# Attention and MLP block on one core: a written-out order of all work, w1 scaled in place, and k's subtractions on GpSimd

## The chip, the cores and the metric

One core of one Trainium2 chip runs the whole kernel. The metric is device microseconds from launch to end. The engines are PE (TensorE, matmuls and transposes), DVE (VectorE), ACT (ScalarE), POOL (GpSimd) and SP (SyncE, which here only issues DMAs).

## The reference

```python
# q, k, v: [8 batches, 8 heads, 576 rows, 64], float32
q_s = softmax(q, over the 64 columns)
k_s = softmax(k, over the 576 rows)
kv  = einsum('bhsd,bhse->bhde', k_s, v)
x   = einsum('bhsd,bhde->bhse', q_s, kv)      # rearranged to [8, 576, 512]
xn  = (x - mean(x)) / sqrt(var(x) + 1e-6) * g # over the 512 columns
out = x + relu(xn @ w_ch1) @ w_ch2            # w_ch1 [512, 2048], w_ch2 [2048, 512]
```

## The kernel before, in words

**Tiles.** Each batch has 576 rows: four tiles of 128 (J = 4) and 64 rows left over. The left-over rows of two batches share one tile, tile number 4, which is treated with the odd batch. The MLP runs in nine chunks of 512 rows: chunk 0 to 7 for the four full tiles of each batch, chunk 8 for the left-over tiles of all eight.

**One batch (`Side`).** `load_k`, `load_v`, `load_q` and the left-over loads bring 1 MB each, plus 128 KB for left-over rows. For k: `kmax` and `kmaxl` take the maximum over rows within a partition (DVE), `kar` reduces it over partitions (POOL, L182), `ksub` subtracts it in place (two large instructions of 128x1024 and a small one of 64x512, DVE, L200), `kexp` takes the exponential (ACT, L213). `vcast` brings v to bf16 (L100). `pkv` multiplies them (PE, L316) and `kvb` divides by the column sums, which come from a column of ones in v (DVE, L325 and L328). For q: `qmax`, `qsub` (DVE, L262, L267), `qexp` (ACT, L272), a transpose, by PE (`qT`, `qTe`) for batches 0 and 1 and by a DMA transpose (`qTd`, L306) later, and the row sums (`zq`, or `zpe` and `zrec` on PE and DVE for batches 0 and 1). `po` multiplies q by kv (PE, L340), `x` scales by the row sums (DVE, L363), `xn` subtracts the mean, `sq` sums squares (ACT, L394), and `xT` with `xTe`, or the DMA transpose `xTd` (L419), gives x transposed.

**g.** In batches 0 and 1 `xTe` multiplies by g when it leaves PSUM (L413). From batch 2 on `xn` is two DVE instructions: L375 scales the sum to a mean, L376 subtracts it and multiplies by g, which `g_bc` holds on all partitions.

**One chunk.** `l1` is 64 matmuls into 16 blocks (`ph`, L449, and `l1_part`, L463, in smaller pieces for chunks 0 and 1), `relu` moves each block to `hT` (ACT, L455, L470), `l2` adds 64 matmuls into four results (`pc`, L505), `put` scales by the row's 1/std and adds x (DVE, L515), `store` writes it out. Four PSUM tiles serve `mm_ps` (ph, pc), four serve `sm_ps` (everything of the batches).

**Order.** All work is a list of tasks with needs. A planner in the kernel file (`dues`, `forward`) gives each task a due time from set costs and a table of shifts, and writes them in a fixed order per engine. All loads and stores but the last store go through SP's queue, in order; weights go through POOL's queue (`load_w1` L428, `load_w2` L432), each of four parts of w1 and w2 being one DMA. Two gates hold SP's queue: `gate` is a tiny DMA that reads w1's second part, so batch 1's loads stand behind its landing; the second reads w2's last part, and loads of later batches stand behind it. `hold` on POOL waits for batch 1's v before w2 is asked for. Batch 0 takes q in two halves (`HALVED`).

Of the kernel before, what the change touches and what calls it, by code (L numbers as in the profile page):

```python
# [13 lines left out]
FP32 = mybir.dt.float32  # L14
# [7 lines left out]
def kernel(  # L22
# [24 lines left out]
    HALVED = (0,)  # L47
    FIRST_DMA = 2
    ZPE = 2
    EARLY_KL = (("kll", 0), ("kl", 0, 1))  # L50
    WARM = 30
    G0 = 1
# [18 lines left out]
    g_bc = const.tile([P, DM], FP32)  # L71
    gate_sb = const.tile([1, 16], BF16)
    hold_sb = const.tile([1, 16], FP32)
# [19 lines left out]
    xm_ab = const.tile([P, B, J + 1], FP32)  # L93
# [12 lines left out]
    def by_dma(m, j):  # L106
        return m >= FIRST_DMA or j == J

    lefts = {}

    def left_over(ring, tag, src, m):

        if (tag, m // 2) not in lefts:
            lefts[tag, m // 2] = ring.tile([P, H, D], FP32, tag=tag, name=tag)
        nc.sync.dma_start(
            lefts[tag, m // 2][rows(m)], src[m, :, SM:, :].transpose([1, 0, 2])
        )

    class Side:
# [6 lines left out]
        def load_kl(self):  # L126
            left_over(kin, "kl", k, self.m)

        def load_k(self, part, parts):
            if part == 0:  # L130
                self.kt = kin.tile([P, H, J * D], FP32, tag="kt")
            hn = H // parts
            hs = slice(hn * part, hn * part + hn)
            src = k[self.m, :, :SM, :].rearrange("h (p j) d -> p h (j d)", j=J)
            nc.sync.dma_start(self.kt[:, hs], src[:, hs])

        def load_v(self):
            src = v[self.m, :, :SM, :].rearrange("h (p j) d -> p h (j d)", j=J)
            self.vt = vin.tile([P, H, J * D], FP32, tag="vt")
            nc.sync.dma_start(self.vt, src)  # L140

        def load_vl(self):
            left_over(vin, "vl", v, self.m)

        def load_q(self, part):
            if part == 0:
                self.qt = qin.tile([P, H * J * D], FP32, tag="qt")
            if self.halved:
                n = H * 2 * D
                src = q[self.m, :, part * 2 * P:(part + 1) * 2 * P, :]  # L150
                nc.sync.dma_start(
# [3 lines left out]
            else:  # L155
                src = q[self.m, :, :SM, :].rearrange("h (p j) d -> p h (j d)", j=J)
                nc.sync.dma_start(self.qt.rearrange("p (h e) -> p h e", h=H), src)

        def load_ql(self, b):
            left_over(qin, "ql", q, b)  # L160

        def kmax(self, hs):
# [4 lines left out]
            nc.vector.tensor_tensor(  # L167
                kmx[:, hs], kt[:, hs, :2 * D], kt[:, hs, 2 * D:], op=ALU.max
            )
            nc.vector.tensor_tensor(  # L170
# [3 lines left out]
        def kmaxl(self, hs):  # L174
            m = self.m
            kmx, r = self.kmx, rows(m)
            nc.vector.tensor_tensor(  # L177
# [192 lines left out]
        def xn(self, eng, j):  # L370

            xt, xs = self.xs[j]
            if by_dma(self.m, j):
                xm = xm_ab[:, self.m, j:j + 1]
                nc.vector.tensor_scalar_mul(xm, in0=xs, scalar1=INV)  # L375
                nc.vector.scalar_tensor_tensor(  # L376
                    xn_ab[:, j], in0=xt, scalar=xm, in1=g_bc,
                    op0=ALU.subtract, op1=ALU.mult,
                )
            elif eng is nc.scalar:  # L380
# [17 lines left out]
        def xT(self, j):  # L398
            pxt = self.pxt[j] = sm_ps.tile([P, KO1, P], BF16, tag="sm", name="pxt")
            for c in range(KO1):  # L400
                nc.tensor.transpose(
                    pxt[:, c, :], xn_ab[:, j, c * P:(c + 1) * P], ident
                )

        def _xnT(self, j):
            m = self.m
            return (
                xnT_ab[:, self.sl, :, j * P:(j + 1) * P] if j < J
                else xnTl[:, :, (m // 2) * P:(m // 2 + 1) * P]
            )  # L410

        def xTe(self, eng, j):
            eng.tensor_tensor(  # L413
                self._xnT(j), self.pxt[j], g_sb[:, :, None].to_broadcast([P, KO1, P]),
                op=ALU.mult,
            )
# [12 lines left out]

    def load_w2(g4):  # L430
        s = slice(4 * g4, 4 * g4 + 4)
        nc.gpsimd.dma_start(w2_sb[:, s], w2_src[:, s, :])  # L432

    def gate(what, c):

        src = w1_sb[:1, 0, c * DM:c * DM + 16] if what == "w1" else w2_sb[:1, 4 * c, :16]
        nc.sync.dma_start(gate_sb, src)

    def hold():

        nc.gpsimd.tensor_copy(hold_sb, side[1].vt[:1, 0, :16])
# [78 lines left out]
    def store(ci, ti):  # L520
        if ci in HALVED:
            dst = out[ci, (ti // 2) * 2 * P:(ti // 2 + 1) * 2 * P, :]
            nc.sync.dma_start(dst.rearrange("(p j) c -> p j c", j=2)[:, ti % 2, :], ots[ti])
        elif ci < B:
            dst = out[ci, :SM, :].rearrange("(p j) c -> p j c", j=J)
            nc.sync.dma_start(dst[:, ti, :], ots[ti])
        else:
            for b in (2 * ti, 2 * ti + 1):
                nc.sync.dma_start(out[b, SM:, :], ots[ti][rows(b)])
# [4 lines left out]


    PE, DV, AC, PO, SP = "pe", "dve", "act", "pool", "sp"
    ENG = {PE: nc.tensor, DV: nc.vector, AC: nc.scalar, PO: nc.gpsimd, SP: nc.sync}
    RING = {"mm": 4, "sm": 4, "ot": 4}
    LATE = {PE: 0.25, DV: 0.12, AC: 0.12, PO: 0.12, SP: 0.1}
    START = {SP: 1.0, AC: 1.0, PO: 4.0}  # L540
    COLD = 25.0
    HOLD = 3.0
    EARLY = 14
    FIRST, SECOND, PERIOD = 20.0, 52.0, 29.7
    TT, CAST, KAR = 1, 2, 3
    SHIFT = {
        ("qmax", 0, 2): 1.8, ("qsub", 0, 2): 10.5, ("relu", 0, 1, 3): 20.8,
        ("relu", 0, 3, 2): 9.2, ("x", 0, 3): -9.0, ("zq", 0, 1): 20.5, ("kexp", 1, 0): 12.9,
        ("ksub", 1, 0): 10.4, ("ksub", 1, 1): 16.3, ("po", 1, 1): -3.4, ("po", 1, 3): -2.8,
        ("put", 1, 0): 40.7, ("put", 1, 1): 41.6, ("put", 1, 3): 9.5, ("qll", 1, 1): -80.7,  # L550
        ("qmax", 1, 2): 22.9, ("relu", 1, 4, 2): 10.2, ("relu", 1, 5, 0): 9.4,
        ("relu", 1, 5, 2): 120.4, ("relu", 1, 6, 0): 51.3, ("relu", 1, 6, 2): 9.8,
        ("relu", 1, 7, 2): 19.9, ("x", 1, 4): -154.5, ("xT", 1, 1): -16.6, ("xn", 1, 2): 26.9,
        ("zq", 1, 4): 115.1, ("kl", 2, 0): -39.6, ("qexp", 2, 2): -6.4, ("qmax", 2, 2): 13.8,
        ("qsub", 2, 0): -2.4, ("qsub", 2, 2): -26.6, ("relu", 2, 1): 61.2, ("relu", 2, 12): 117.0,
        ("relu", 2, 7): 30.4, ("store", 2, 1): 31.4, ("store", 2, 2): 38.1, ("vl", 2): -23.4,
        ("x", 2, 3): 22.2, ("zq", 2, 0): -13.4, ("kexp", 3, 0): -21.5, ("kl", 3, 0): -30.4,
        ("kmaxl", 3, 0): 6.4, ("ksub", 3, 2): -23.6, ("kvb", 3): -29.9, ("qll", 3, 0): -169.6,
        ("qmax", 3, 2): 59.3, ("relu", 3, 10): 81.4, ("relu", 3, 7): 19.6, ("relu", 3, 8): 124.9,
        ("vl", 3): -7.0, ("zq", 3, 0): 58.2, ("kexp", 4, 0): -17.7, ("kl", 4, 0): 42.8,  # L560
        ("kmax", 4, 0): 75.7, ("ksub", 4, 2): -8.6, ("ql", 4, 0): -52.7, ("qsub", 4, 0): 66.6,
        ("vl", 4): 60.6, ("vll", 4): -50.7, ("kmax", 5, 0): -41.7, ("kmaxl", 5, 0): -34.8,
        ("ksub", 5, 1): -45.8, ("ql", 5, 0): 45.7, ("vl", 5): 44.4, ("kl", 6, 0): 4.8,
    }
    tasks = []

    class Task:
        def __init__(self, due, fn, args, eng, need, after, takes, frees, mlp, move, grain, port):
            self.due, self.fn, self.args, self.eng = due, fn, args, eng
            self.need, self.after, self.takes, self.frees = need, after, takes, frees  # L570
            self.mlp, self.move, self.grain, self.port = mlp, move, grain, port
            self.users = []
            self.n = len(tasks)

    def task(
        fn, args, eng, *need, after=None, takes=None, frees=None, mlp=False, move=None, due=None,
        grain=1.0, port=0,
    ):
        flat = []
        for x in need:  # L580
            flat.extend(x if isinstance(x, (list, tuple)) else [x])
        need = [x for x in flat if x]
        after = [x for x in (after if isinstance(after, list) else [after]) if x]
        t = Task(due, fn, args, eng, need, after, takes, frees, mlp, move, grain, port)
        tasks.append(t)
        return t

    def long(t, e, at):
        w = t.eng[e]
        return 2 * w if e == PE and at < COLD else w  # L590

    def lag(t):

        return (1.9 if t.move else 0.12 if t.on == PE else 0.05)

    class Wire:

        def __init__(self):
            self.now, self.rings = 0.0, {e: [] for e in ENG}

        def run(self, until, rings):
            now = self.now
            while now < until:
                heads = [r for r in rings.values() if r]
                if not heads:
                    return
                now = max(now, min(r[0][2] for r in heads))
                if now >= until:
                    return
                going = [r for r in heads if r[0][2] <= now + 1e-9]  # L610
                whole = sum(r[0][0].grain for r in going)
                dt = min(r[0][1] * whole / r[0][0].grain for r in going)
                for r in heads:
                    if r[0][2] > now + 1e-9:
                        dt = min(dt, r[0][2] - now)
                dt = min(dt, until - now)
                now += dt
                for r in going:
# [548 lines left out]
```

## Time and profile before

| what | value |
|---|---|
| time, median of 3 runs | 308.18 us (307.34 to 309.3) |
| profiled execution, time | 308.83 us |
| profiled execution, span | 307.0 us |
| PE, DVE, ACT, POOL busy | 284.8, 210.2, 161.0, 42.2 us |
| mean granted PE clock | 0.972 |
| DMA moved | 49.90 MB, mean 163 GB/s |

Times inside the profile count from the start of the span. A wait is put down to the work that released the waiting instruction. Where a line of the profile ends in a bracket, it gives idle time before the instruction and its releaser. A suffix "q" (SPq, POOLq) is an engine's queue issuing a DMA.

### The profile page before, as it was taken

The page shows a single profiled execution, that of the slowest core. Times are in us where ns is not written, and L with a number is a line of the kernel's source. Part 1 is how long each engine was busy: PE and PEld are TensorE (multiplying, and loading weights), DVE is VectorE, ACT ScalarE, POOL GpSimd, SP SyncE. Part 2 cuts the span into 40 slices and gives each one's busy share as a digit, 9 for nine tenths or more (in the row PEclk, how much of TensorE's full clock was granted, in tenths as well). Part 3 has the DMA queues.
Part 4 walks back from the last instruction along what each step waited for, and adds up shares of the span by engine and source line. Part 5 has one row for each costly group of instructions (what it writes and reads, how often), then busy time and mean ns, then how long its engine had stood idle before and what let it go on. Part 6 is the DMA issues. An engine that isn't in the chain of part 4 may idle for free.

```text
span 307.0 us, 5187 instructions
## 1 busy us (share of the span) xinstructions
PE 284.8 (93%) x2002; PEld 153.9 (50%) x2030; DVE 210.2 (68%) x347; ACT 161.0 (52%) x288; POOL 42.2 (14%) x46
## 2 busy tenths in 40 slices
PE   6659959999989998999999999999999999999995
PEld 2239955568544444445444545444544444444444
DVE  5893898789888896998889889988984500020012
ACT  1444746459543974286837763777477136106500
POOL 2600150023113000233016100060000000000000
PEclk9956998999999999999999999999999999999999
DMA  6999998999999995599398369945142310010023
GB/s 207 251 184 260 259 182 134 296 275 323 188 240 169 283 213 126 143 270 339 93 275 202 68 160 222 287 55 137 70 87 51 105 69 0 34 70 34 0 65 74
DMA packets 79545, 49.90 MB, mean 163 GB/s; under 512 B 44960, under 2 KB 74912, under 8 KB 79520
## 3 DMA queue, kind: packets, MB, share of 16 engines
q1 hardware_dynamic: 75136, 45.24, 62.1%
q0 software_dynamic: 4224, 4.19, 8.7%
q8 instruction: 16, 0.26, 0.4%
q10 hardware_dynamic: 160, 0.13, 0.2%
q14 instruction: 9, 0.07, 0.1%
HBM read 36.96 MB, written 9.44 MB: 151 GB/s over the span
## 4 chain that ended last, share of the span: by engine, by line
PE 76%; DMA 13%; DVE 3%; ACT 2%; issue 1%; SPq 1%; POOL 1%; ACTq 0%
PE pc L505 36%; PE ph L449 31%; DMA vt<-in_v_dram 4%; PE ph L463 3%; DMA qT_sb<-eq_sb 3%; DMA w_sb<-in_moe_w_ch_dram 3%; DMA kt<-in_k_dram 2%; PE pot L340 2%; DVE v_ab L100 2%; PE pk L316 1%; PE pc L481 1%; ACT ek_ab L213 1%; DMA xnT_ab<-xn_ab 1%; ACT hT L455 1%; POOL km L182 1%
## 5 line engine op out<-in xcount | busy, mean ns | idle before, releaser
L505 PE MATMUL pc<-w_sb,hT 128*128 128x512 bf16 x543 | 124.6, 381 | 1.3 <-issue 0.7
L455 ACT ACTIVATE hT<-ph 128x512 bf16<-128x512 f32 x112 | 66.0, 597 | 58.5 <-PE ph L449 58.1
L449 PE MATMUL ph<-xnT_ab,w_sb 128*128 128x512 bf16 x375 | 84.6, 379 | 0.8 <-DMA xnT_ab<-xn_ab 0.3
L505 PEld LDWEIGHTS <-hT 128*128 128x128 bf16 x560 | 53.8, 98 | 61.7 <-issue 1.4
L449 PEld LDWEIGHTS <-w_sb 128*128 128x128 bf16 x448 | 43.4, 98 | 51.9 <-issue 0.8
L515 DVE SCALAR_TENSOR_TENSOR ot<-pc,rstd,x_ab 128x512 f32<-128x512 f32 x32 | 23.9, 750 | 39.5 <-PE pc L505 37.6
L463 PE MATMUL ph<-xnT_ab,w_sb 128*128 128x128 bf16 (+1 forms) x384 | 31.4, 246 | 1.0 <-DVE xnT_ab L413 1.0
L394 ACT ACTIVATE xsq<-x_ab,xs_ab 128x512 bf16<-128x512 bf16 x32 | 23.0, 718 | 14.8 <-DVE x_ab L363 13.8
L463 PEld LDWEIGHTS <-w_sb 128*128 128x128 bf16 x384 | 29.0, 103 | 2.8 <-issue 0.9
L272 ACT ACTIVATE eq_sb<-qt 128x1024 bf16<-128x1024 f32 (+1 forms) x17 | 17.1, 1005 | 20.3 <-DVE qt L267 18.0
L363 DVE SCALAR_TENSOR_TENSOR x_ab<-pot,rq 128x512 bf16<-128x512 f32 x32 | 21.0, 686 | 7.3 <-PE pot L340 6.9
L100 POOL CAST v_ab<-vt 128x1024 bf16<-128x1024 f32 x12 | 13.1, 1123 | 87.7 <-DMA vt<-in_v_dram 87.7
L470 ACT ACTIVATE hT<-ph 128x512 bf16<-128x512 f32 x32 | 18.3, 593 | 9.1 <-PE ph L463 8.8
L182 POOL PARTITION_ALL_REDUCE km<-kmx x9 | 17.0, 1886 | 36.2 <-DVE kmx L177 34.1
L267 DVE TENSOR_TENSOR qt<-qt,qm 128x1024 f32<-128x1024 f32 (+1 forms) x17 | 20.4, 1208 | 0.3
L262 DVE TENSOR_REDUCE qm<-qt 128x16 f32<-128x1024 f32 (+1 forms) x17 | 19.2, 1146 | 0.6 <-DMA qt<-in_q_dram 0.5
L376 DVE SCALAR_TENSOR_TENSOR xn_ab<-x_ab,xm_ab,g_bc 128x512 bf16<-128x512 bf16 x24 | 18.0, 752 | 0.8
L515 DVE SCALAR_TENSOR_TENSOR ot<-pc,rstd,xl 128x512 f32<-128x512 f32 x3 | 2.3, 750 | 21.9 <-PE pc L505 21.9
L200 DVE TENSOR_TENSOR kt<-kt,km 128x1024 f32<-128x1024 f32 x14 | 17.0, 1237 | 0.1
L213 ACT ACTIVATE ek_ab<-kt 128x1024 bf16<-128x1024 f32 x14 | 14.5, 1052 | 1.6 <-DVE kt L200 1.5
L277 DVE TENSOR_REDUCE sumq<-eq_sb 128x16 f32<-128x1024 bf16 x12 | 14.5, 1204 | 0.1
L449 PE MATMUL ph<-xnTl,w_sb 128*128 128x512 bf16 x62 | 13.9, 379 | 0.1
(73 smaller groups left out, 199.3 us busy)
## 6 DMA issues: line engine op xcount, KB each, us to landing
vt<-in_v_dram SPq DMA_DIRECT2D x8, 1024.0 KB, 9.4
out_dram<-ot SPq DMA_DIRECT2D x32, 256.0 KB, 2.9
kt<-in_k_dram SPq DMA_DIRECT2D x7, 1024.0 KB, 8.1
qt<-in_q_dram SPq DMA_DIRECT2D x7, 1024.0 KB, 8.9
w_sb<-in_moe_w_ch_dram POOLq DMA_DIRECT2D x8, 512.0 KB, 10.0
kt<-in_k_dram SPq DMA_DIRECT2D x2, 512.0 KB, 5.4
kl<-in_k_dram SPq DMA_DIRECT2D x8, 128.0 KB, 6.9
vl<-in_v_dram SPq DMA_DIRECT2D x8, 128.0 KB, 6.6
```

The lines of the kernel that those rows point to most:

```text
L100: eng.copy(dst, src) if eng is nc.scalar else eng.tensor_copy(dst, src)
L182: nc.gpsimd.partition_all_reduce(self.km[:, hs], self.kmx[:, hs, :D], P, bass_isa.ReduceOp.max)
L262: nc.vector.tensor_reduce(t, self._q(a, n), axis=AX.X, op=ALU.max)
L267: eng.tensor_tensor(x, x, t[:, :, :, None].to_broadcast([P, n, H, D]), op=ALU.subtract)
L363: nc.vector.scalar_tensor_tensor(xt.rearrange("p (h d) -> p h d", h=H), in0=self.pot[j], scalar=-1.0, in1=rq[:, :, None].to_broadcast([P, ...
L394: nc.scalar.activation(xsq, xt, AF.Square, bias=xs, scale=-float(DM), accum_out=s)
L449: nc.tensor.matmul(ph, w1_sb[:, ko, m * P:(m + 1) * P], src[:, ko, :], start=(ko == 0), stop=(ko == KO1 - 1),)
L455: nc.scalar.activation(hT[:, m, :], phs[m], AF.Relu)
L463: nc.tensor.matmul(ph[:, i], w1_sb[:, ko, m * P:(m + 1) * P], xnT_ab[:, ci % 2, ko, t * P:(t + n) * P], start=(ko == 0), stop=(ko == KO1 - 1),
L470: nc.scalar.activation(hT[:, c * (4 // n):(c + 1) * (4 // n), t * P:(t + n) * P], phs[c, t], AF.Relu)
L505: nc.tensor.matmul(pcs[ti], hT[:, ko, ti * P:(ti + 1) * P], w2_sb[:, ko, :], start=(ko == 0), stop=(ko == KO2 - 1),)
L515: nc.vector.scalar_tensor_tensor(ots[ti], in0=pcs[ti], scalar=rstd[:, ci, ti:ti + 1], in1=xt, op0=ALU.mult, op1=ALU.subtract,)
```

## The change

The planner, its costs and its shifts go. The order is a written-out list, `PROGRAM`, of task names with the engine where there is a choice; `write_all` follows it word for word. Both gates, `hold`, `g_bc` and the two halves of batch 0's q go. ACT may issue loads and stores too. In chunk 0 g is applied as before, when x leaves PSUM; once chunk 0 has read a part of w1, `scale_w1` multiplies that part by g in place (four instructions of 128x512 for each of four parts, two parts on DVE and two on POOL), and from batch 1 on `xn` is one instruction on DVE (L385's form) or ACT (L381's form), and x leaves PSUM by a plain copy. Batch 2's x is transposed by PE instead of DMA, two tiles to one PSUM tile, as in batch 1. From batch 1 on k's subtractions stand on POOL, but for one large one of batch 1, and one large and the small one of batch 7, which stay on DVE. No cast of v is left on DVE.

```diff
-    HALVED = (0,)
-    FIRST_DMA = 2
+    HALVED = ()
+    Q_DMA, X_DMA = 2, 3
...
         def xn(self, eng, j):
             xt, xs = self.xs[j]
-            if by_dma(self.m, j):
-                xm = xm_ab[:, self.m, j:j + 1]
-                nc.vector.tensor_scalar_mul(xm, in0=xs, scalar1=INV)
-                nc.vector.scalar_tensor_tensor(
-                    xn_ab[:, j], in0=xt, scalar=xm, in1=g_bc,
-                    op0=ALU.subtract, op1=ALU.mult,
-                )
-            elif eng is nc.scalar:
+            if eng is nc.scalar:
...
+        def xTe(self, eng, a, n):
+            dst = self._xnT(a, n).rearrange("p c (j t) -> p c j t", j=n)
+            src = self.pxt[a].rearrange("p j c t -> p c j t")
+            if self.m == 0:
+                b = g_sb[:, :, None, None].to_broadcast([P, KO1, n, P])
+                eng.tensor_tensor(dst, src, b, op=ALU.mult)
+            else:
+                copy(eng, dst, src)
...
+    def scale_w1(eng, c):
+        for ko in range(KO1):
+            w = w1_sb[:, ko, c * DM:(c + 1) * DM]
+            if eng is nc.scalar:
+                eng.activation(w, w, AF.Identity, scale=g_sb[:, ko:ko + 1])
+            else:
+                eng.tensor_scalar_mul(w, in0=w, scalar1=g_sb[:, ko:ko + 1])
...
-    def gate(what, c):
-        src = w1_sb[:1, 0, c * DM:c * DM + 16] if what == "w1" else w2_sb[:1, 4 * c, :16]
-        nc.sync.dma_start(gate_sb, src)
-
-    def hold():
-        nc.gpsimd.tensor_copy(hold_sb, side[1].vt[:1, 0, :16])
...
+    W1S = (PO, AC, DV)
+    KSUB, KSUBL = (DV, PO), (DV, PO)
+    LD = (SP, AC)
+    PROGRAM = """
+        kl.0.0@SP kl.0.1@SP ql.0.0@SP kll.0 vl.0@SP vll.0 kl.1.0@SP kll.1@SP ql.1.0@SP vl.1@SP
+        kmax.0.0 kmax.0.1 kmaxl.0.1 kmaxl.0.0 kar.0.1 w1l.0 ksub.0.1 vc.0.2@AC w1l.1 kar.0.0
+        qmax.0.0 kexp.0.1 qsub.0.0 w1l.2 ksub.0.0 g w1l.3 qexp.0.0 w2l.0 vc.0.1@AC qT.0.0 qmax.0.1
...
+    def write_all():
+        for word in PROGRAM.split():
+            name, _, on = word.partition("@")
+            name, *numbers = name.split(".")
+            t = T[(name, *map(int, numbers))]
+            on = on or t.eng[0]
+            assert on in t.eng and not t.written and all(x.written for x in t.need), word
+            t.fn(ENG[on], *t.args)
+            t.written = True
```

The order by engine, as far as chunk 1, read out of the list. A name has the batch or chunk first; "kl", "ql", "vl" are loads, "kll", "vll" left-over loads, "w1l", "w2l" weight loads, "w1s" is `scale_w1`, "vc" is `vcast`.

```
SP:   kl.0.0 kl.0.1 ql.0.0 vl.0 kl.1.0 kll.1 ql.1.0 vl.1 kl.2.0 kll.2 vll.4 ql.2.0 vl.2 vll.2
      kl.3.0 kll.3 ql.3.0 qTd.2.0 qTd.2.1 ...
POOL: kar.0.1 w1l.0 w1l.1 kar.0.0 w1l.2 w1l.3 w2l.0 vc.0.0 kar.1.0 w2l.1 ksub.1.2 vc.1.2 ksub.1.0
      w2l.2 w2l.3 vc.1.1 w1s.0 w1s.2 kar.2.0 ksub.2.2 ksub.2.0 ksub.2.1 vc.2.2 vc.2.1 vc.2.0 kar.3.0 ...
ACT:  kll.0 vll.0 vc.0.2 kexp.0.1 g qexp.0.0 vc.0.1 kexp.0.0 qexp.0.1 qTe.0.0 qexp.0.2 ...
DVE:  kmax.0.0 kmax.0.1 kmaxl.0.1 kmaxl.0.0 ksub.0.1 qmax.0.0 qsub.0.0 ksub.0.0 ... kmax.1.0 xTe.0.2
      kmaxl.1.0 xTe.0.3 ksub.1.1 w1s.1 qmax.1.0 qmax.1.2 qsub.1.0 qsub.1.2 w1s.3 qTe.1.0 kvb.1 ...
      qsub.2.0 xTe.1.2 qmax.2.2 zq.2.0 qsub.2.2 kmax.3.0 kmaxl.3.0 kvb.2 ...
PE:   ... xT.0.1 l1.0.0.0 l1.0.1.0 l1.0.0.1 l1.0.1.1 xT.0.2 l1.0.2.0 l1.0.2.1 xT.0.3 l1.0.0.2
      l1.0.1.2 l1.0.1.3 l1.0.3.0 ... l1.0.2.3 l2.0.0 l2.0.1 l2.0.2 l2.0.3 qT.1.0 l2.0.4 l2.0.5
      pkv.1.0 pkv.1.1 zpe.1.0 qT.1.2 ... l2.0.15 l1.1.0.0 l1.1.1.0 po.1.3 ... xT.1.2 ... pkv.2.0 ...
```

## The prediction

> **What bounds the kernel now.** I read the engine totals first, then time slices, then PE's waits, then the chain that ended last, then the groups.
>
> ```profile
> PE 284.8 (93%) x2002; PEld 153.9 (50%) x2030; DVE 210.2 (68%) x347; ACT 161.0 (52%) x288; POOL 42.2 (14%) x46
> ...
> PEclk9956998999999999999999999999999999999999
> ```
>
> PE is busy 93% of a 307.0 us span, and its clock is below full only in the third to seventh slice (about 15 to 29 us, again near 47 us). So the question is where PE's missing 22 us lie. Windows of the trace (PE busy is the number behind the first span, DVE the third pair, then ACT and POOL):
>
> ```profile
> 10.00:20.00 10.00, 5.48 (x69) 3.23 (x67) 9.81 (x16) 5.98 (x9) 5.06 (x5) 0.75 1.02 196
> 20.00:30.00 10.00, 7.84 (x90) 7.66 (x89) 5.91 (x14) 4.48 (x8) 0.00 (x0) 0.57 1.19 250
> ...
> 40.00:50.00 10.00, 6.09 (x69) 4.43 (x67) 8.70 (x8) 5.68 (x8) 2.92 (x3) 0.83 1.18 188
> ...
> 80.00:100.00 20.00, 18.24 (x130) 8.63 (x131) 16.53 (x31) 7.60 (x18) 5.99 (x5) 1.00 1.16 183
> 100.00:120.00 20.00, 18.56 (x133) 9.01 (x135) 16.75 (x31) 15.48 (x29) 0.61 (x1) 1.00 1.09 222
> ```
>
> PE loses 4.5 + 2.2 us before 30 us, 3.9 us in 40 to 50, and 1.8 and 1.4 us in 80 to 120; later windows lose 0.1 to 0.7 us per 20. The waits of PE over the whole span, of which only the qT_sb one lies in the steady part:
>
> ```profile
> PE ptr L296 <- ACT eq_sb L272: 5.3, 3, 3.7
> PE pot L340 <- DMA qT_sb<-eq_sb: 2.7, 4, 1.3
> ```
>
> The chain (start, duration, what) gives the fixed points:
>
> ```profile
> 23.23 0.61 SPq L437
> ...
> 25.31 11.78 DMA vt<-in_v_dram
> 37.11 4.49 DVE v_ab L100 x2
> ...
> 45.10 1.07 ACT eq_sb L272
> ...
> 65.55 10.49 PE ph L463 x96
> ...
> 299.82 3.51 PE pc L481 x32
> ```
>
> Batch 1's loads stand behind a gate that waits for w1 (23.23). v lands at 37.1, its two casts hold DVE for 4.49 us, q's row maximum and exponential come behind them, and PE, done with chunk 0's first layer at 42.5, waits 3.7 us for the exponential and runs at half clock until 49. Chunk 1 starts on PE at 65.55. From there to 303.33 PE works 237.8 us, some 4 us of it stalls; 3.7 us of last output follow.
>
> **The change, part by part.**
>
> *First layer of chunk 0 starts later.* Batch 0's q comes as one load ahead of v, and the left-over rows and g come from ACT's queue. GpSimd reduces half 1 of k first, then writes two w1 descriptors, then reduces half 0. The walk from the rows: kmax of half 1 ends about 10.5 as before; its reduction (1.06, the first L182) ends at 11.5; two w1 descriptors of 0.82 follow to 13.1; reduction of half 0 (1.06) ends at 14.2. From 11.5 DVE subtracts half 1 (1.21 + 0.41), then q's maximum (0.66 + 0.69) and half 0 (1.62), with 0.5 of waiting for that reduction: 16.6. ACT does kexp half 1 (1.06 + 0.40, to 14.7), issues g (2.01 us where SP issued it; I take 2.0, bounds 0.5 and 2.0), then qexp (0.63), a v cast (1.03) and kexp half 0 (1.46): 19.8. Then pkv 1.1, kvb 1.03, po 0.6, x 0.77, xn 0.35, transposes 0.6, xTe 0.69 and issue gaps: first layer at 25.9 instead of 23.2, **+2.7**.
>
> *That layer itself.* Before it took 23.2 to 42.5, with qT, zp, pot and pxt of tiles 1 to 3 mixed in. In the new order most of these precede it; left are 16 parts of 0.91, two x transposes of 0.22 and about 3 us at half clock and gaps: 18.1, ending at 44.0. It needs w1's four parts at about 25.9, 27.8, 32 and 36.5. Before, with nothing beside it, the second part landed at 23.2, 9.84 us after issue. Now k, q and v of batch 1 (3.4 MB) flow from 14.5 on in the other queue. From 23 to 37 DMA moved 210 to 274 GB/s, against 339 in its best slice, so shared w1 comes slower: not at all as lower bound, twice the latency (second part at 32.7) as upper. I take 1.4 times, just in time for each part, plus **0.5**.
>
> *The stall at 42.5 goes.* The v casts of batch 1 leave DVE for ACT and GpSimd; row maxima of q now stand on DVE behind one subtraction, q lands about 33, and four second-layer blocks (3.5 us) are put between the first layer and qT. qexp waits on ACT only for the last relu (45.8), qT would run at 47.9: no stall. What is late next is w2: without gates its last two parts are issued at about 39 instead of 42, are wanted at 55 and 59, and landed before by 52.4, so 3 us and more are spare even beside batch 2's loads. Second layer 13.8, plus qT, zp, pkv, pot and pxt 3.2, plus 0.5 small gaps: chunk 1 at about 44.5 + 17.5 = 62.0, **3.5 earlier** than 65.55.
>
> *w1 scaled in place.* 16 multiplications of 128x512 bf16: eight on DVE at 0.354 (the row of L385) = 2.8 us; eight on GpSimd, not in the trace, between 0.6 (its cast of 64x512) and 1.1 (its 128x1024 cast) each. I take 0.8, 6.4 us in all, from about 42 to 49. The covers are the 13.8 us of chunk 0's second layer; they are needed at 62 and 65. Uncovered, each part would cost 3.2. Price 0.
>
> *DVE's relief.* 28 xn pairs (0.147 + 0.752 = 0.90) become 19 of 0.354 on DVE and 9 of 0.718 on ACT: 25.2 - 6.7 = 18.5 off DVE. Casts of v: 6.8 off, 3.1 of them waiting for GpSimd's descriptors. Subtractions of k moved to GpSimd: 12 large x 1.237 + 6 small x 0.683 = 18.9. With the w1 products DVE falls from 210 to about 169 us. DVE is not the bound, so this buys only waits: of the 4 us of stalls behind 65.55 I credit **2.5**, bounds 0 and 4.
>
> *GpSimd's subtractions.* No two-input GpSimd operation is in the trace. Lower bound 1.12, its cast of the same shape (one input); upper 3.9, below. Two inputs of that shape read one after the other are two casts: I take 2.1, small ones 1.05, so 5.3 per batch; with reduction 1.8 and casts 2.8 GpSimd has 10 of 29 us of a batch. In the walk batch 2's last subtraction ends at 65.9, its exponential at 71, pkv is due at 74; kvb may be 3.1 us late before po waits. Price 0 at 2.1.
>
> The two engines do get in each other's way, as these rows show (GpSimd's reduction of the same half tile, alone and beside DVE's subtraction; two casts of 0.61 begun behind DVE's subtraction of q; two DVE casts that take 0.73 alone):
>
> ```profile
> 6.65 1.06 POOL L182 PARTITION_ALL_REDUCE km<-kmx  x1 [4.81 <-DVE kmx L177]
> ...
> 10.55 1.97 POOL L182 PARTITION_ALL_REDUCE km<-kmx  x1 [2.84 <-DVE kmx L177]
> ...
> 91.19 2.24 POOL L100 CAST v_ab<-vl 64x512 bf16<-64x512 f32 x2 [6.21 <-DMA vl<-in_v_dram]
> ...
> 37.11 4.49 DVE L100 CAST v_ab<-vt 128x1024 bf16<-128x1024 f32 x2 [0.66 <-DMA vt<-in_v_dram]
> ```
>
> 0.9, 1.0 and 3.1 us of waiting; 3.9 is one stalled cast. [...]
>
> *New work.* Batch 2's x transposes move from DMA to PE: four times 0.22 (L401 x4 in the chain) = **+0.9**. Two x transposes and one pot of batch 1 (0.45 + 0.22) now fall behind chunk 1's start: **+0.7**, counted there. [...] On SP, v of batch 3 stands behind a qT transpose that waits for an exponential; it should land at 91.5 with pkv wanted at 97.
>
> *Sum.* Span 62.0 + 237.8 + 0.9 + 0.7 - 2.5 + 0.5 + 3.7 = 303.1. The profiled run took 308.83 for a span of 307.0, so 1.8 lie around it: 304.9. That run is 0.65 above the median 308.18: **304.3**.
>
> **Rivals.**
>
> *Weights too late.* Without gates, w1 and batch 1 share the DMA. For it: the DMA share is already above 1.0 in 20 to 40. Against: before, w1's own issue had a slow start, and batch 1 is not needed until 36. At twice the latency PE waits 4.9 us for w1's second part, less 0.5 already counted: 304.3 + 4.4 = **308.7**, no change.
>
> *Slower: subtractions hold DVE.* In batch 2, q's subtraction on DVE meets the subtractions on GpSimd; behind it on DVE stand a maximum, a sum, k's maximum of batch 3 and kvb, and PE's po waits for kvb. With e us more per large subtraction, DVE is 2.5 e late against 3.1 of slack: it decides from 3.35 us per subtraction. At 3.9, 1.4 us in each of six batches: 304.3 + 8.4 = **312.7**. For it: the 3.9 us cast. Against: casts beside DVE's subtractions cost 0.3 (DVE 0.98 for 0.68 at 136.4) to 1.0.
>
> *All stalls go.* g costs ACT 0.5, w1 is on time, the 4 us all vanish: 304.3 - 1.5 - 0.5 - 1.5 = **300.8**. For it: DVE at 169 us. Against: new orders bring waits of their own.
>
> **How the numbers follow.** Forecast 0.50, weights late 0.18, subtractions 0.22, all stalls gone 0.10. A measurement here tells about 1% from no change: 305.1 and 311.3 are the limits. The forecast's own range, 302 to 307, is three quarters below 305.1: faster 0.38 + 0.10 = 0.48. Same 0.12 + 0.14 of the weights + 0.02 of the subtractions = 0.28. Slower 0.04 + 0.20 = 0.24. The range 300 to 313 goes from the last rival to the slower one.
>
> **What would show it.** Right: PE's first L463-type matmul near 26, no wait of PE on eq_sb near 43, chunk 1 on PE at 61 to 63, DVE busy 165 to 173, GpSimd's subtraction 1.7 to 2.7 us. Wrong: a PE wait on w_sb between 28 and 40 (weights), GpSimd's subtraction over 3.3 us with PE waiting on kv_ab in several batches (slower rival), or relus that wait behind an ACT-issued load.

## Result: slower by 13.5%, and the profile after

The changed kernel takes 350.19 us (median of 4 runs, 347.17 to 350.88) against 307.76 for the kernel before on the same chip (307.0 to 309.3): a ratio of 1.135 [1.127, 1.143]. The forecast was 304.3 with a range of 300 to 313. The profiled execution took 350.1 us for a span of 348.3.

Engine totals and granted clock from the page of the changed kernel, to be held against the same two lines of before:

```profile
PE 290.4 (83%) x2019; PEld 154.1 (44%) x2046; DVE 174.6 (50%) x290; ACT 165.9 (48%) x303; POOL 92.7 (27%) x74
...
PEclk9999998976999699998999579999999999999999
```

DVE fell by 36 us, as it was meant to, and no engine is full: PE is down to 83%. Its clock, which before was below full only ahead of 50 us, now dips near 57, 78, 117, 161 and 200 us (slices of 8.7 us). Windows of the changed kernel (same columns as in the prediction) show where PE stands still:

```profile
60.00:80.00 20.00, 10.28 (x70) 6.45 (x70) 6.48 (x10) 1.01 (x1) 7.53 (x5) 0.84 0.25 68
...
100.00:120.00 20.00, 13.67 (x70) 6.59 (x70) 7.90 (x14) 7.41 (x14) 8.86 (x5) 0.83 0.79 193
...
180.00:200.00 20.00, 8.36 (x54) 3.96 (x54) 1.93 (x3) 4.29 (x7) 9.88 (x7) 0.76 0.47 134
```

In 60 to 80 us PE, DVE and ACT together are busy for 17.8 of 60 engine microseconds, and the DMA share is 0.25. GpSimd, the engine that would have to be at fault, is busy for only 7.53 of 20. So everyone waits for something that no row counts as busy. PE's waits name the branches:

```profile
PE idle L930 <- POOL ident masks.py:199: 11.9, 1, 11.9
PE ph L454 <- ACT hT L461: 11.4, 1, 11.4
PE pk L310 <- ACT ek_ab L207: 9.5, 2, 8.3
PE pxt L389 <- ACT xn_ab L368: 6.5, 2, 6.3
PE pk L310 <- POOL v_ab L94: 3.3, 2, 3.1
```

The first of them stands ahead of all work, before PE's warm-up matmuls on the identity matrix (`ident`). None of these is a wait on DVE, and none on the transfer of a weight (those are 2.5 and 1.7 us in all). GpSimd in order of time (start, duration, and in the bracket the idle time before and its releaser; L176 is the reduction over partitions, L194 k's subtraction, L428 the product of w1 with g):

```profile
11.25 0.19 POOL masks.py:197 MEMSET ident<- 128x128 bf16 x1 [10.82 <-issue]
...
43.39 1.72 POOL L194 TENSOR_TENSOR kl<-kl,km 64x512 f32<-64x512 f32 x1 [7.46 <-issue]
...
50.82 13.22 POOL L428 TENSOR_SCALAR w_sb<-w_sb,g_sb 128x512 bf16<-128x512 bf16 x8
69.73 2.78 POOL L176 PARTITION_ALL_REDUCE km<-kmx  x1 [5.69 <-issue]
79.29 1.25 POOL L194 TENSOR_TENSOR kl<-kl,km 64x512 f32<-64x512 f32 x1 [6.78 <-issue]
80.51 4.63 POOL L194 TENSOR_TENSOR kt<-kt,km 128x1024 f32<-128x1024 f32 x2
...
93.62 1.80 POOL L176 PARTITION_ALL_REDUCE km<-kmx  x1 [5.95 <-DVE kv_ab L322]
...
130.50 1.81 POOL L176 PARTITION_ALL_REDUCE km<-kmx  x1 [13.46 <-DVE kmx L171]
...
167.15 4.66 POOL L194 TENSOR_TENSOR kt<-kt,km 128x1024 f32<-128x1024 f32 x2 [10.83 <-issue]
```

The thing to see is the idle time: before the first subtraction behind a reduction, and before the first reduction behind a subtraction or product, GpSimd stands still. In between, where the same kind follows itself, there is no gap. The order on GpSimd goes from reduction to subtraction seven times (gaps of 6.8 to 10.8 us) and back six times (four gaps of 5.7 to 6.1 us): 13 changes of kind. The other two ways back, at 130.50 and 232.47, are longer because the reduction also waited for k's maximum (`kmx`), which DVE finished 0.1 to 0.2 us before it started; there the change was hidden behind that wait.

The releaser in the bracket needs care. Seven of the 13 gaps are put down to "issue", that is, to nothing that the profile shows. Four more, of 6 to 7 us, carry the name of an engine's instruction that the GpSimd instruction does not need: the reduction at 93.62 reads `kmx`, which was ready at 92.4, and not `kv_ab`. And "issue" alone proves no change of kind: the kernel before has one such gap, ahead of a cast, which starts as PE's product of k and v, the reader of the buffer `v_ab`, ends (105.83 + 0.83):

```profile
105.83 0.83 PE L316 MATMUL pk<-v_ab,ek_ab 128*64 128x65 bf16 x40
...
106.78 0.61 POOL L100 CAST v_ab<-vl 64x512 bf16<-64x512 f32 x1 [9.98 <-issue]
```

So the gaps are a suspicion here, and the experiments have to settle it. A further 10.82 us stand at the start, ahead of GpSimd's first instruction of the body (11.25); they hold PE's warm-up matmuls and bring the first layer to 27.9 us instead of 24.9 in the kernel e1 below.

What that does in batch 2, in ACT's and PE's order of time:

```profile
80.57 0.63 ACT L207 ACTIVATE ek_ab<-kl 64x512 bf16<-64x512 f32 x1 [16.36 <-POOL kl L194]
81.11 1.05 ACT L461 ACTIVATE hT<-ph 128x512 bf16<-128x512 f32 x2
```

k's exponential waits 16.36 us for GpSimd's subtraction, and chunk 1's relus stand behind it on ACT. PE's first layer has no free PSUM tile and waits 11.4 us for the first of them. DVE has nothing to do either: it idles 14.70 us up to 85.55.

### The profile page after: what moved, and what is told of

It reads as the page before. It is cut to its first block, busy times and chain, and to the rows that moved or that the text cites. A ratio compares the mean times of both kernels' runs of the same rounds, so it can differ in the third digit from the quotient of the medians.

```text
span 348.3 us, 5169 instructions
## 1 busy us (share of the span) xinstructions
PE 290.4 (83%) x2019; PEld 154.1 (44%) x2046; DVE 174.6 (50%) x290; ACT 165.9 (48%) x303; POOL 92.7 (27%) x74
## 4 chain that ended last, share of the span: by engine, by line
PE 48%; issue 17%; POOL 12%; DVE 9%; DMA 7%; ACT 3%; SPq 2%; POOLq 0%; ACTq 0%; DVEq 0%
PE ph L440 23%; PE pc L496 20%; POOL kt L194 3%; POOL w_sb L428 3%; DMA ql<-in_q_dram 2%; POOL kl L194 2%; DMA vl<-in_v_dram 2%; DMA out_dram<-ot 2%; DMA qt<-in_q_dram 2%; POOL v_ab L94 1%; DVE x_ab L357 1%; POOL km L176 1%; DVE qt L261 1%; SPq L300 1%; PE pk L310 1%
## 5 line engine op out<-in xcount | busy, mean ns | idle before, releaser
L496 PE MATMUL pc<-w_sb,hT 128*128 128x512 bf16 x546 | 126.5, 387 | 3.3 <-DMA w_sb<-in_moe_w_ch_dram 2.5
L446 ACT ACTIVATE hT<-ph 128x512 bf16<-128x512 f32 x112 | 64.2, 595 | 74.4 <-PE ph L440 69.5
L440 PE MATMUL ph<-xnT_ab,w_sb 128*128 128x512 bf16 x372 | 90.7, 389 | 3.7 <-ACT hT L446 2.4
L506 DVE SCALAR_TENSOR_TENSOR ot<-pc,rstd,x_ab 128x512 f32<-128x512 f32 x32 | 23.3, 740 | 66.3 <-PE pc L496 42.5
L454 PE MATMUL ph<-xnT_ab,w_sb 128*128 128x128 bf16 (+1 forms) x384 | 31.1, 242 | 13.1 <-ACT hT L461 11.4
L176 POOL PARTITION_ALL_REDUCE km<-kmx x9 | 15.7, 1744 | 83.6 <-DVE kmx L171 59.7
L454 PEld LDWEIGHTS <-w_sb 128*128 128x128 bf16 x384 | 27.5, 100 | 15.8 <-issue 11.6
L194 POOL TENSOR_TENSOR kt<-kt,km 128x1024 f32<-128x1024 f32 x12 | 28.0, 2339 | 17.8 <-issue 10.8
L207 ACT ACTIVATE ek_ab<-kl 64x512 bf16<-64x512 f32 x7 | 4.4, 626 | 42.2 <-POOL kl L194 42.1
L381 ACT ACTIVATE xsq<-x_ab,xs_ab 128x512 bf16<-128x512 bf16 x32 | 22.9, 715 | 0.7 <-ACT ek_ab L207 0.5
L261 DVE TENSOR_TENSOR qt<-qt,qm 128x1024 f32<-128x1024 f32 (+1 forms) x17 | 22.3, 1322 | 0.1
L461 ACT ACTIVATE hT<-ph 128x512 bf16<-128x512 f32 x32 | 18.2, 595 | 6.5 <-PE ph L454 5.8
L310 PE MATMUL pk<-v_ab,ek_ab 128*64 128x65 bf16 x320 | 8.5, 204 | 12.8 <-ACT ek_ab L207 9.5
L930 PE MATMUL idle<-kv_ab,ident 128*128 128x512 bf16 x30 | 8.9, 468 | 11.9 <-POOL ident masks.py:199 11.9
L194 POOL TENSOR_TENSOR kl<-kl,km 64x512 f32<-64x512 f32 x6 | 8.3, 1387 | 37.3 <-issue 37.2
L94 POOL CAST v_ab<-vt 128x1024 bf16<-128x1024 f32 x14 | 16.2, 1170 | 1.2 <-DMA vt<-in_v_dram 1.0
```

The lines of the kernel that those rows point to most:

```text
L94: eng.copy(dst, src) if eng is nc.scalar else eng.tensor_copy(dst, src)
L176: nc.gpsimd.partition_all_reduce(self.km[:, hs], self.kmx[:, hs, :D], P, bass_isa.ReduceOp.max)
L194: eng.tensor_tensor(a, a, b, op=ALU.subtract)
L261: eng.tensor_tensor(x, x, t[:, :, :, None].to_broadcast([P, n, H, D]), op=ALU.subtract)
L381: nc.scalar.activation(xsq, xt, AF.Square, bias=xs, scale=-float(DM), accum_out=s)
L440: nc.tensor.matmul(ph, w1_sb[:, ko, m * P:(m + 1) * P], src[:, ko, :], start=(ko == 0), stop=(ko == KO1 - 1),)
```

## The experiments

The theory: GpSimd pays 6 to 11 us for each change between the reduction and the elementwise operations with two inputs or a factor for each partition. What GpSimd does in that time no trace shows; the theory is of the gap alone. Rivals: the subtractions and products are themselves too slow ("slow subtraction") or hold DVE; the new order with its loads is bad ("order"); the weights come late.

**e1_sub_on_dve**: the changed kernel, with everything but GpSimd's two new jobs kept.

```diff
-  ksub.*@PO      w1s.0@PO w1s.2@PO
+  ksub.*@DV      w1s.0@AC w1s.2@AC
```

By the theory the time is 299 to 308 us here, and GpSimd's first operation comes near 1 us. Slow subtractions would give about the same time; e2 tells the two apart.

> The changed kernel, with k's subtractions of all batches on DVE and the two w1 products of GpSimd on ACT, so that GpSimd does reductions, casts and weight loads as before the change. [...] Rival 'order': the written-out order without gates is itself bad, the subtractions are bystanders; then 335 us or more. [...]

Measured 300.07 us (299.95 to 300.62), ratio 0.974 [0.970, 0.979]. The order, the missing gates and w1 scaled in place together make the kernel faster than before by 2.6%; the whole loss sits in what GpSimd was given. It is also the version that beats both kernels.

```profile
PE 282.4 (95%) x2019; PEld 152.5 (51%) x2046; DVE 185.1 (62%) x308; ACT 171.5 (58%) x311; POOL 43.9 (15%) x48
```

PE has the same 2019 instructions. Between the two spans (348.3 and 298.2) lie 50.1 us: PE idles 57.9 us against 15.8, which is 42.1, and is busy 8.0 longer at its lower clock (mean 0.945 against 0.982). So the waits cost about a fifth more than their length.

**e2_no_reduction**: the changed kernel, all subtractions and products still on GpSimd, with the reduction over partitions replaced by a copy, and the kernel's `load_library` line left out.

```diff
-  nc.gpsimd.partition_all_reduce(self.km[:, hs], self.kmx[:, hs, :D], P, bass_isa.ReduceOp.max)
+  nc.gpsimd.tensor_copy(self.km[:, hs], self.kmx[:, hs, :D])
```

By the theory 300 to 312 us, with every subtraction and product kept. If these are too slow themselves, or hold DVE, 335 or more.

> The changed kernel with all its GpSimd subtractions and w1 products, but the reduction of k's maximum over the partitions is left out (GpSimd copies its input instead, so each partition keeps its own maximum). [...] 'Order': still 335 us or more.

Measured 308.82 us (306.46 to 311.57), ratio 1.001 [0.997, 1.005]. GpSimd in order of time:

```profile
42.94 12.80 POOL L426 TENSOR_SCALAR w_sb<-w_sb,g_sb 128x512 bf16<-128x512 bf16 x8
55.69 0.60 POOL L176 COPY km<-kmx 128x512 f32<-128x512 f32 x1
56.38 1.26 POOL L192 TENSOR_TENSOR kl<-kl,km 64x512 f32<-64x512 f32 x1
57.61 4.64 POOL L192 TENSOR_TENSOR kt<-kt,km 128x1024 f32<-128x1024 f32 x2
```

The same work, of the same length, runs without a gap, and 41.4 of the 50 us are gone. Most of the loss is the alternation, not the instructions. **e8_no_reduction_sub_on_dve** is the control, e1 with the same replacement.

> Control for the kernels without the reduction: k's subtractions on DVE, w1 products on DVE and ACT, GpSimd copies in place of reducing. It tells what leaving out the reduction is worth by itself: 299 to 300.5 us, against 300.1 with it. Anything below 298 would mean that the reduction itself was on the path, and that the kernels without it look too good by as much.

Measured 299.95 us, ratio 0.972 [0.967, 0.977], 0.1 us from e1. Leaving out the reduction gains nothing that can be told where nothing alternates with it.

**e3_before_plus_changes**: the kernel before, its subtractions on DVE, with 13 changes and hardly any work added.

```diff
+  # Side.kar, behind the reduction, batches 1 to 7
+  nc.gpsimd.tensor_tensor(tiny, tiny, tiny, op=ALU.subtract)   # 1 x 16
```

> The kernel before, with one tiny two-input GpSimd subtraction (1x16) added behind the reduction of each batch from batch 1 on; all real subtractions stay on DVE. [...] 315 to 335 us, with GpSimd idle gaps of 6 us around each tiny subtraction, and the first GpSimd operation near 11 us. 'Slow subtraction' or 'order': 308 us, within 1%.

Measured 325.19 us (322.97 to 328.59), ratio 1.054 [1.048, 1.060]. The profiled execution took 328.59 us, and its lines are read for GpSimd's gaps alone:

```profile
91.51 0.20 POOL L187 TENSOR_TENSOR tiny<-tiny 1x16 f32<-1x16 f32 x1 [9.84 <-issue]
...
117.12 0.38 POOL L187 TENSOR_TENSOR tiny<-tiny 1x16 f32<-1x16 f32 x1 [7.46 <-issue]
```

A subtraction of 16 numbers has the same gap of 7 to 10 us before it. It reads and writes only its own tile, so it has nothing of another engine to wait for. Seventeen microseconds are lost although only v's casts, the weight requests, the next reduction and the start of the kernel (first operation at 9.52) stand behind these gaps here, with k's subtractions on DVE.

**e4_before_plus_one_at_end**: the kernel before, with one such tiny subtraction as the last instruction on GpSimd.

If what GpSimd ran last reaches into the next execution, its first operation comes near 11 us there, and the time is 312 to 316.

> The kernel before, with one tiny two-input GpSimd subtraction as GpSimd's very last instruction, where nothing waits for it. [...] If each execution starts afresh, or the idle 10 us at the start of the changed kernel has another cause (its DMAs come earlier), 308 us and GpSimd's first operation near 0.9 us.

```profile
8.36 0.20 POOL masks.py:197 MEMSET ident<- 128x128 bf16 x1 [7.92 <-issue]
```

Without it, GpSimd's first instruction of the body stands at 0.91 with 0.46 of idle time (before and e1 alike). So in e4 an instruction at the end of the program moved the beginning by 7.45 us, which the author reads as a change of kind from one execution to the next. Having both kinds in the program is not enough for it: e5 and e6 below have both, end with reductions and casts, and start at 0.89. The time, however, is 308.43, ratio 1.002 [0.999, 1.006]: the 4 to 8 us on top did not come. The first reduction moved from 6.65 to 9.83, but both halves were reduced by 12.1 (12.5 before), and GpSimd asked for w1 at 11.97 against 12.40. The first layer still began 1.8 us later (25.02 against 23.22); PE's warm-up matmuls end later and the mean granted clock is 0.987 instead of 0.972. That the clock pays for the 1.8 us is read from these rows, not tested.

**e5_w1_on_gpsimd**: e1 with only the w1 products back on GpSimd: two changes, no subtraction.

```diff
-  w1s.0@AC w1s.2@AC
+  w1s.0@PO w1s.2@PO
```

By the theory GpSimd idles 6 to 10 us ahead of the products and 6 behind, batch 2's reduction ends about 15 us later, pkv of batch 2 waits for it, and the time is 306 to 313. The products' own 13 us alone would leave 300 to 302.

> The changed kernel with all of k's subtractions on DVE, but the eight w1 products still on GpSimd. [...]

Measured 316.07 us (315.76 to 316.52), ratio 1.024 [1.019, 1.030], 16.0 above e1 and well over what was expected. GpSimd, DVE and PE's wait:

```profile
50.64 12.77 POOL L428 TENSOR_SCALAR w_sb<-w_sb,g_sb 128x512 bf16<-128x512 bf16 x8 [7.55 <-PE pot L334]
69.28 1.80 POOL L176 PARTITION_ALL_REDUCE km<-kmx  x1 [5.87 <-issue]
...
71.12 2.98 DVE L194 TENSOR_TENSOR kl<-kl,km 64x512 f32<-64x512 f32 x1 [14.06 <-POOL km L176]
...
PE ph L454 <- DVE ot L506: 15.1, 1, 15.1
```

The change to the products took 7.55 us (the bracket names PE; in e2 the same products follow the same cast at 42.94 without a gap), the products 12.8 from 50.6 on, the change back 5.87, and batch 2's reduction came at 69.28 instead of 53.88. DVE's subtraction waited 14 us for it, chunk 0's last results (`put`) stood behind that on DVE and held PE's PSUM tiles. One wait of 15.1 us is nearly the whole loss. The theory had the late reduction right and the place of the wait wrong: it was not at pkv of batch 2.

**e11_changed_w1_on_act**: the other way round, the changed kernel with those products on ACT and all 13 changes left.

> [...] The 13.2 us of products no longer stand between the second change and batch 2's reduction, so PE's wait of 11.4 us for batch 2 (at 81.7 in the changed kernel) shrinks to 0 to 3 us; the changes of batches 3 to 6 stay: 335 to 343 us against 350.2. If the products were the main cost and the changes a small one: under 325.

Measured 339.03 us (336.62 to 342.13), ratio 1.099 [1.091, 1.107], 11.2 below the changed kernel. The wait of 11.4 us is down to 0.2; beside it a new one of 3.0 us stands, for an `xn` on DVE (e7 comes back to such instructions). The other long waits stand.

**e6_three_batches**: the changed kernel with the subtractions of batches 4 to 7 back on DVE, which leaves six changes and none at the start. If each change weighs alike, 320 to 328 us.

> [...] If one single place (180 to 200 us, where PE idled 11.6 us) did most of the harm: under 315.

Measured 325.29 us (324.65 to 326.01), ratio 1.054 [1.048, 1.060]. With e1 and the changed kernel this is a dose: 0, 6 and 13 changes give 300.1, 325.3 and 350.2 us. The work moves along with the changes (the last step also brings ten subtractions and the gap at the start), so the dose alone would not tell them apart; e2 and e3 do.

**e7_no_reduction_w1_on_act**: e2, which has both the subtractions and the w1 products on GpSimd, with the products on ACT. If GpSimd's unbroken run is what holds DVE (the row of 7.32 us below), e2's wait of 5.0 us falls under 1 us and the time is 302 to 305.

> [...] In the kernel with both on GpSimd (308.8) GpSimd ran without a gap from 42.9 to 64.8, and one DVE instruction of 0.35 us took 7.3 us until that run ended; PE waited 5.0 us for what stood behind it. [...] If each subtraction alone costs its length on the path: still 306 or more.

Measured 304.88 us (303.0 to 309.11), ratio 0.993 [0.989, 0.998]: 3.9 below e2, 4.9 above e8. So without any change of kind the products on GpSimd cost 3.9 us and the subtractions 4.9. The runs of e2 and e7 spread over 5 to 6 us each, so either share may be off by some 2 us. What they do is seen in e2, on DVE:

```profile
56.63 7.32 DVE L370 TENSOR_SCALAR xn_ab<-x_ab,xs_ab 128x512 bf16<-128x512 bf16 x1
```

This normalization of one tile takes 0.35 us elsewhere. It began behind the start of GpSimd's small subtraction at 56.38 and ended at 63.95, after both large ones and some of the casts. PE waited 5.0 us for the `put` behind it. In e7 the same instruction took 3.42, and PE's wait for the `put` was 1.1. It is not the only place. In e7 another instruction of this form took 6.46 us:

```profile
102.40 6.46 DVE L370 TENSOR_SCALAR xn_ab<-x_ab,xs_ab 128x512 bf16<-128x512 bf16 x1
```

In e8, with the subtractions on DVE, no instruction of this form took over 0.81 us.

**e10_xn_on_act**: e2 with that one instruction, `xn.1.2`, on ACT.

> The kernel without the reduction, everything else of the changed kernel on GpSimd (308.8), with one xn (batch 1, tile 2) on ACT in place of DVE. It was the DVE instruction of 0.35 us that took 7.32 us while GpSimd ran subtractions and casts without a gap. 'DVE's fast form starves until GpSimd's run ends': PE's wait of 5.0 us for what stood behind it goes, 303 to 305 us. 'The next DVE instruction would be held as well': 307 or more.

Measured 305.9 us (303.1 to 307.59), ratio 0.997 [0.993, 1.001], between the two expectations, and not clearly below e2 (1.001 [0.997, 1.005]). The next instruction of the same form was held instead:

```profile
59.35 5.62 DVE L370 TENSOR_SCALAR xn_ab<-x_ab,xs_ab 128x512 bf16<-128x512 bf16 x1
```

Just ahead of it q's row maximum (57.31, 1.21 us) and x (58.61, 0.69 us) ran at their normal length. PE's wait there was 2.7 in place of 5.0.

**e9_xn_first**: e1 with batch 2's last subtraction put behind `xn.1.3` on DVE, to gain PE's wait of 1.2 us at that place.

> The kernel with k's subtractions on DVE and w1 products on DVE and ACT (300.1), with one move: batch 2's last large subtraction goes behind xn of batch 1's tile 3 on DVE, where PE waited 1.2 us for that xn (64.1). 298.5 to 299.5 us if that wait was worth its length; 300.1 if the time returns at the next wait.

Measured 300.64 us (299.97 to 301.07), ratio 0.976 [0.972, 0.981]. The wait went from 1.2 to 0.4, the time did not move. No gain can be told, so e1 stays the best.

## Why the prediction was wrong

**The step that failed** is "GpSimd's subtractions". Its size for one subtraction was good: 2.1 taken, 2.34 measured, inside the 1.12 to 3.9. What the step lacked is a term ahead of the instruction. "GpSimd has 10 of 29 us of a batch" added reduction, subtractions and casts as if they followed each other freely; with a change of 7.8 us on the mean towards the subtraction and one of 6 us back they take about 24, and, worse, the change lies in series between the reduction and the subtraction, ahead of k's exponential. The walk that let batch 2's last subtraction end at 65.9 was 19 us out: it ended at 85.1, behind three changes and products twice as long as taken. The trace before could not show the term: GpSimd held no operation with two inputs there. The range did not hold it because the bounds were put on the instruction and not on its being another kind of instruction than its neighbour. None of the rivals named such a gap. Nor did the signs of being right test it: a subtraction of 1.7 to 2.7 us and no wait on `eq_sb` near 43 both came true in a kernel that was 15% slower than forecast. What GpSimd does in a gap no run shows; the runs show the gap (5.7 to 10.8 us in the changed kernel) and what brings it.

**"w1 scaled in place, price 0"** failed twice. A product takes 1.65 us (13.22 for 8), not 0.8, and it is of the other kind: e5 puts it at 16.0 us alone, e11 at 11.2 within the changed kernel. The cover named, chunk 0's second layer, did cover the products; what it did not cover was the reduction of batch 2 queued behind them.

**The rival "subtractions hold DVE"** named an effect that the rows show (an `xn` of 0.35 us took 7.32 in e2) and had the wrong point of decision. It should have decided from 3.35 us for a subtraction; at 2.34 the subtractions already cost about 4.9 us where GpSimd runs without gaps (e7 against e8), which the rows put down to DVE instructions held over several GpSimd instructions and not to longer subtractions. In the changed kernel itself no `xn` on DVE took over 1.71 us; how much of its loss is this rival's, no run tells.

**"Weights too late"** is 1.7 and 2.5 us of PE's waits in the changed kernel and not the cause. The 0.5 us in the sum for loads and stores issued by ACT is shown by no run as a term of its own: in e1, which issues them the same way, PE's waits hold none for a relu, and the changed kernel's issues took at most 0.80 us each.

**What was right** is seen in e1, which has everything but GpSimd's new jobs. The stall at 42.5 went: PE is busy 16.85 of the 17.08 us from 40 to 57.08. From chunk 1's start to PE's end it took 237.4 us (57.08 to 294.46); the prediction's terms for that stretch, 237.8 + 0.9 + 0.7 - 2.5 + 0.5, give 237.4. That the two agree to 0.1 us is luck in part: e1 keeps k's subtractions on DVE, which is busy 185.1 us and not the 169 of the forecast, and PE idles 2.6 us in that stretch, where the terms leave 2.0. Chunk 1 started at 57.1, not 62.0: first layer at 24.9 instead of 25.9 (its issue of g took ACT 0.48, not 2.0), that layer 14.9 instead of 18.1 (the 3 us allowed for half clock and gaps were not needed), the rest 17.3 instead of 18.0. Thus e1 measured 300.07, just under the rival "all stalls go" at 300.8.

**The account of the changed kernel**, from one kernel to the next: 350.2 with changes of kind, 308.8 without (e2, -41.4), 304.9 with the products off GpSimd (e7, -3.9), 300.0 with the subtractions off it (e8, -4.9). The shares depend on the order of the steps, because each removed wait uncovers another: the products are worth 3.9 us here and 11.2 when they are the first to go (e11).

## What to carry to other kernels

Before work is moved to GpSimd, list the kinds of instruction in its order and count how often the kind changes; in the changed kernel a change between the reduction and the subtraction or product cost 5.7 to 10.8 us where the instructions themselves took 0.6 to 2.8, lay in series with what it separated in 11 of 13 places (in the other two the reduction waited for its input anyway), and showed in the profile only as idle time, put down to "issue" or to an engine that the instruction did not need. To tell such a gap from a hidden wait, put in an instruction that needs nothing, as e3 does. Give an engine whole runs of one kind, or leave the second kind elsewhere: here the reduction on GpSimd cost nothing that could be told (e8 against e1), and the subtractions and products without the reduction about 9 of the 50 us (e2 against e8). A price for an instruction that the trace lacks needs a bound for its start as well as for its length.

## What the runs showed of the hardware

- A change of kind on GpSimd, between the reduction over partitions and the subtraction or the product, shows as a gap of 5.7 to 10.8 us in these traces, whatever the size of the instruction behind it (1x16 or 128x1024). Towards the subtraction it is the longer one (6.8 to 10.8 in the changed kernel, against 5.7 to 6.1 back). v's casts took part in no change: they ran without such a gap behind either kind (at 85.10 behind a subtraction, at 234.34 behind a reduction). Why one gap is 6.8 and another 10.8 stays open.
- One subtraction as GpSimd's last instruction of the program came with 7.92 us of idle time ahead of its first instruction of the body, against 0.46 without it (e4, before).
- The DVE instruction `xn` (128x512 bf16), 0.35 us elsewhere, took 7.32 (e2), 6.46 (e7) and 5.62 us (e10) where GpSimd had the subtractions. In e2 it ran from 56.63 to 63.95, beside GpSimd instructions that followed each other without a gap from 56.38 to 64.84, and did not get done between one of them and the next.
